# The first layer of one more token group from seven quarter products, and one filler pace for the attention loop

## The chip, the core and the metric

The kernel runs on one NeuronCore of a Trainium2 chip. Its engines run their own instruction streams and meet through semaphores: TensorE (PE in the profile; PEld is its weight loads), VectorE (DVE), ScalarE (ACT), GpSimd (POOL) and SyncE (SP), which here only issues transfers. Products are summed in PSUM, eight banks of 128 partitions by 512 fp32 numbers; VectorE and ScalarE carry results from there to SBUF. The metric is the device time of one execution in microseconds.

## What is computed

Causal attention with a bias per head, then a mixer over tokens (of rank 32) and a mixer over channels, with residuals:

```python
scores = scale * np.matmul(q, k.transpose(0, 1, 3, 2))      # 8 batches, 8 heads, 576 x 576, D = 64
cum = np.cumsum(np.maximum(s, 0.0), axis=-1)
bias = -(cum[:, :, :, None] - cum[:, :, None, :])
scores = np.where(causal, -1e9, scores + np.minimum(bias, 0.0))
x = softmax(scores) @ v                                     # then (batch, 576, 512)
u = x + ((x.transpose(0, 2, 1) @ U) @ V).transpose(0, 2, 1) # U 576 x 32, V 32 x 576
out = u + np.maximum(u @ w_ch1, 0.0) @ w_ch2                # 512 -> 2048 -> 512
```

## The kernel before

**Attention** goes by pairs of heads, n = 0 to 31, four pairs to a batch (b = n // 4). For a pair, `scores` makes the transposed scores in three two-bank PSUM tiles and a small one, ScalarE takes their exponentials (L446, L458, L464), VectorE masks the diagonal blocks (L372), and `values` multiplies with V and divides (L501, L502). From the third batch on, the loop over n interleaves, in the order in which the code is written out, the transposed inputs of pair n+1 (`transposes`, `part_pair`), the scores of pair n and the values of pair n-1.

**`seqmix(b)`** is the token mixer of a batch: 20 small products (L522), a cast, a transpose (L535), a cast, four products against V (L567) and one more group (L592); VectorE adds the residual and writes `uT` (L547). For batches 2 to 6 it runs in the second pair of the next batch (n = 13, 17, 21, 25, 29); for batch 7 after the loop.

**The channel mixer** goes by groups of 512 tokens, g = 0 to 8 (NG = 9), which run across batches. `chanmix(g)` is a generator: sixteen steps of the first layer (`hidden`: four 128x512 products at L662, then a relu at L1044), and then the second layer, `outputs_by_quarters`, in fourteen steps of eight 128x256 products (L720). The second layer is done as a 2x2 block product with seven quarter products instead of eight (p1 to p7, Strassen's way in Winograd's form); sums of weight quarters (B_1 to B_4) and of hidden quarters (A_1 to A_4, L698, in `first_sums` and `total`) are made by VectorE, as are the sums of the products (L734).

**Filler.** The generators wait in the list `fill`. `step_fill` is called after each piece of attention work and adds `pace[1]` to a count; each time this reaches 16, one step of the first generator is issued. `fill_with(n)` issues n steps at once. So pace 12 means 12 steps for 16 calls. There are eight calls to a pair. The loop runs at pace 11 in batch 2, 12 in batches 3 to 5 and 10 in 6 and 7.

**The tail.** After the loop the steps go on until group 6's first layer is issued. Then the attention pools of PSUM are closed, and three others open: two banks for `pwork`, one each for two tiles of the second layer, and four for `hidden_by_quarters`. This function makes the first layer, too, from seven quarter products, for groups 7 and 8: for each of four parts e, 14 slots of which seven do work, four 128x256 products each (L952). Parts overlap: slots 8, 12 and 13 of e stand among the first slots of e+1. ScalarE copies partial sums out and applies relus (L967, L971, L988, L999, L1002, L1006), VectorE adds (L965). Sums of weight quarters (W_1 to W_4, in `first_weight_sums`, L922) are made once, in group 6's first layer; sums of token quarters (`token_sums`, L934 to L937) for each group. Second-layer steps of the group before are placed between the slots by the list `fills`, fourteen for each of groups 7 and 8.

**Order.** TensorE's and GpSimd's instructions stand in the order of the code; on the other engines the scheduler orders them, except where `placed` pins a VectorE instruction behind the one before it. Each engine takes its instructions in that order, so one that waits holds what is behind it.

Of the kernel before, what the change touches and what calls it, by code (L numbers as in the profile page):

```python
# [41 lines left out]
def kernel(  # L42
# [652 lines left out]

    def total(dst, a, b, op, k4):
        at = (slice(None), slice(4 * k4, 4 * k4 + 4))
        nc.vector.tensor_tensor(dst[at], a[at], b[at], op=op)  # L698

# [6 lines left out]
    def outputs_by_quarters(g, hT, u_sd):  # L706
# [146 lines left out]
        for i in halves:  # L853
            product(p6, A_2, B_2, i)
            if i == 1:
                total(A_4, A12, A_2, ALU.subtract, 0)
            yield
        add(U2, U2, p6)
        p5 = bank()
        for i in halves:  # L860
            product(p5, A_1, B_1, i)
            total(*((A_4, A12, A_2), (A_3, A11, A21))[i], ALU.subtract, 1 - i)
            yield
# [3 lines left out]
        for i in halves:  # L867
            product(p3, A_4, B22, i)
            if i == 0:
                o12 = quarter()  # L870
                add_u(o12, o22, 0, 1)
                total(A_3, A11, A21, ALU.subtract, 1)
            yield
# [32 lines left out]

    def first_sum(tile, free):
        return tile.rearrange(free)[:, : 2 * HW].rearrange("p (k n) -> p k n", k=2)

    W_3, W_1, W_4 = (first_sum(slots[i], "p a b -> p (a b)") for i in range(3))  # L910
    W_2 = first_sum(v_slots[2], "p a b c -> p (a b c)")

# [26 lines left out]

    def hidden_by_quarters(u, u_sums, hT, sets):  # L940
        (u11, u21, _, u22), (u_1, u_2, u_3, u_4) = u_quarters(u), u_sums
# [22 lines left out]
        def add(e, r, c, a, b):  # L964
            nc.vector.tensor_tensor(out(e, r, c), a, b, op=ALU.add)  # L965
            if (r, c) == (0, 0):
                nc.scalar.activation(out(e, r, c), out(e, r, c), RELU)  # L967
            elif c == 0:
                both = hT[:, ds(8 + 2 * e, 2), :]
                if sets == 4:  # L970
                    nc.scalar.activation(both, both, RELU)  # L971
                else:
                    nc.vector.tensor_scalar_max(both, both, 0.0)

        parts = {}

        def at(e, slot):
            if not 0 <= e < sets:
                return False
# [11 lines left out]
            if slot == 2:  # L991
                product(p.w, W_3, u_3, e, True)
            elif slot == 3:
                x = two(pwork())
                product(x, W12, u21, e, True)
                add(e, 0, 0, p.p1, x)
            elif slot == 4:
                product(p.y, W_2, u_2, e, False)
                nc.scalar.copy(p.U2, p.y)  # L999
            elif slot == 8:  # L1000
                product(p.y, W_1, u_1, e, False)
                nc.scalar.copy(p.U4, p.y)  # L1002
                add(e, 1, 1, p.U4, p.w)
            elif slot == 12:
                product(p.y, W_4, u22, e, False)
                nc.scalar.activation(out(e, 0, 1), p.y, RELU)  # L1006
            elif slot == 13:
                product(p.w, W22, u_4, e, False)
                add(e, 1, 0, p.U2, p.w)
                if sets == 4 and e in (2, 3):  # L1010
                    first_sums(hT, e == 2)
            return True

        for e in range(sets + 1):
            for slot in range(7):
                late = slot in (1, 5, 6)
                if at(e - late, slot + 7 * late):
                    yield
# [14 lines left out]
    def chanmix(g, hT=None, done=0):  # L1033
        u = uT_of.pop(g)
        if g > 0:
            hT = work.tile([128, NF, 512], BF16, tag="hT", name="hT")
            sums = {1: weight_sums, NG - 3: first_weight_sums}.get(g, lambda: iter(()))()
        for nf in range(done, NF):
# [10 lines left out]
            if g > 0 and nf == 3:  # L1049
                u_sd = by_token(u)  # L1050
            if nf == NF - 1:
                expanded.append(g)
            yield
# [25 lines left out]
    fill = []  # L1079
    expanded = []  # L1080
    relu_by = [E.Activation]
# [3 lines left out]
    def step_fill():  # L1085
        pace[0] += pace[1]
        if pace[0] < 16:
            return
        pace[0] -= 16
        if NG - 3 in expanded and not ps_tail:  # L1090
            return
        while fill:
            if next(fill[0], fill) is not fill:
                return
            fill.pop(0)
# [150 lines left out]
    fill.append(chanmix(1))  # L1246
    pace[1] = 11
    for n in range(2 * PB, NP + 2):
        b, hp = divmod(n, PB)
# [4 lines left out]
        mixing = seqmix(b - 1) if hp == 1 and b > FT else iter(())  # L1254
        if b == B:
            fill_with(3)
            for _ in range(3):
                step(mixing)
                fill_with(2)
        if n > 2 * PB and n + 1 < NP:  # L1260
            for at, _ in enumerate((transposes if n + 1 < ZP else part_pair)(n + 1)):
                step_fill()
                if at == 1:
                    step(mixing)
        if 2 * PB + 1 < n < NP:
            for at, _ in enumerate(scores(n, pT_of(n))):
# [5 lines left out]
        for _ in mixing:  # L1272
            fill_with(1)
        if hp == 1 and FT < b < B:
            fill.append(chanmix(b - 1))
            pace[1] = 12 if b < 6 else 10
        if 2 * PB < n <= NP:
            run(values(n - 1, pT_of(n - 1)))
        if 2 <= b < B - 1:
            if b + 1 < ZB:  # L1280
                load_v(b + 1, range(5 if hp == 0 else 0))
            else:
                load_v(b + 1, ((0, 1), (2,), (3,), (4,))[hp])
    pace[1] = 16
    while NG - 3 not in expanded:
        step_fill()
# [4 lines left out]
    ps_t = ctx.enter_context(tc.tile_pool(name="ps_t", bufs=4, space=bass.MemoryType.PSUM))  # L1291
    tail_sums = {}
    tail_sums[NG - 2] = token_sums(
        uT(NG - 2), v_slots[1].rearrange("p a b c -> p (a b c)")
    )
    xT_again = work.tile([128, 4, 640], BF16, tag="xT", name="xT", bufs=1)
    def hidden_plain(u, hT, nfs):
        for at, nf in enumerate(nfs):
            f1 = pwork()
            hidden(f1, u, nf, range(4))  # L1300
            nc.scalar.activation(hT[:, nf, :], f1, RELU)
            yield

    for g, sets, fills in ((NG - 2, 4, (0, 0, 2, 4, 6, 8, 10, 12, 14, 17, 20, 23, 25, 26)), (NG - 1, 4, (1, 3, 5, 7, 9, 11, 13, 16, 19, 22, 25, 25, 26, 26))):
        u = uT_of.pop(g)
        u_sd = by_token(u, True)
        hT = work.tile([128, NF, 512], BF16, tag="hT", name="hT")
        for at, _ in enumerate(hidden_by_quarters(u, tail_sums[g], hT, sets)):
            for _ in range(fills.count(at)):
                step_fill()  # L1310
            if at == 3 and g < NG - 1:
                tail_sums[NG - 1] = token_sums(
                    uT(NG - 1), xT_again.rearrange("p a b -> p (a b)")
                )
        if sets < 4:
            for one in (True, False):
                first_sums(hT, one)
        while fill:
# [35 lines left out]
```

## Time and profile before

| | |
|---|---|
| median of 3 runs | 347.83 us (347.70 to 348.11) |
| the profiled execution, its own time | 347.92 us |
| its span | 346.1 us |
| PE busy | 336.4 us (97%) |
| DVE busy | 260.6 us (75%) |
| ACT busy | 203.9 us (59%) |
| first-layer products L662 | 407 + 16 rows, 104.2 + 3.9 us busy |
| second-layer products L720 (all forms) | about 880 rows, 273 ns each as recorded |
| quarter products L952 of groups 7 and 8 | 224 rows, 272 to 273 ns each as recorded |

[...] A few per cent of the matmul records are missing, which in a timeline looks like a gap of one product's length. "Idle before" is an engine's idle time just before an instruction, with what ended it. Of an engine beside TensorE, idle time costs nothing by itself.

### The profile page before, as it was taken

What the parts mean: (1) busy time and instruction counts of PE and PEld (TensorE: products, weight loads), DVE (VectorE), ACT (ScalarE), POOL (GpSimd) and SP (SyncE); (2) the same over time, 40 slices, a digit from 0 to 9 for tenths busy, and PEclk for the clock granted to TensorE, in tenths of its full rate; (3) what the DMA queues carried; (4) which work ended last, traced back from release to release, by engine and by line L of the source; (5) the groups of instructions that cost most, each with busy time, mean ns of one, the idle gap of its engine ahead of it and who ended that gap; (6) DMA issues with size and microseconds to landing.
All of it is one profiled execution on the core that took longest, in us unless ns stands there. A gap on an engine that the chain in (4) does not pass through costs nothing.

```text
span 346.1 us, 8930 instructions
## 1 busy us (share of the span) xinstructions
PE 336.4 (97%) x3607; PEld 243.7 (70%) x3641; DVE 260.6 (75%) x576; ACT 203.9 (59%) x308; POOL 125.8 (36%) x183
## 2 busy tenths in 40 slices
PE   8999999999999999999999999999999999999996
PEld 4685556656688558865678568865687568888885
DVE  8894756778799668974898469965988597875874
ACT  4786985638850886178624883388552546665710
POOL 7997358848494309431823374000000000000000
PEclk9999999999999999999999999999999999999999
DMA  7999999999999999999999999495025252010022
GB/s 107 154 180 207 182 185 127 160 204 204 148 167 168 203 138 102 134 196 152 117 117 176 176 128 149 109 179 68 14 56 136 57 95 59 30 63 32 30 93 91
DMA packets 169696, 44.09 MB, mean 127 GB/s; under 512 B 154584, under 2 KB 168024, under 8 KB 169656
## 3 DMA queue, kind: packets, MB, share of 16 engines
q0 software_dynamic: 99440, 18.44, 71.0%
q1 hardware_dynamic: 69928, 24.90, 38.5%
q8 instruction: 28, 0.46, 0.6%
q10 hardware_dynamic: 288, 0.20, 0.2%
q14 instruction: 12, 0.10, 0.1%
HBM read 37.25 MB, written 9.70 MB: 136 GB/s over the span
## 4 chain that ended last, share of the span: by engine, by line
PE 81%; DVE 10%; ACT 4%; issue 3%; DMA 1%; SPq 0%; DVEq 0%; ACTq 0%
PE pwork L662 23%; PE pwork L720 13%; PE quarter L720 10%; PE pscore L428 10%; PE pwork L492 8%; PE parts L952 6%; PE pwork L681 3%; DVE uT L547 2%; DVE slot L698 1%; DVE o_sb L734 1%; DMA slot<-hT 1%; PE pwork L952 1%; PE pscore L662 1%; ACT hT L1044 1%; PE pwork L522 1%
## 5 line engine op out<-in xcount | busy, mean ns | idle before, releaser
L662 PE MATMUL pwork<-uT,w_sb 128*128 128x512 bf16 x407 | 104.2, 379 | 1.9 <-ACT pT L464 0.5
L1044 ACT ACTIVATE hT<-pwork 128x512 bf16<-128x512 f32 x107 | 64.8, 610 | 37.5 <-PE pwork L662 36.6
L446 ACT ACTIVATE pT<-pscore 128x1024 bf16<-128x1024 f32 x57 | 57.5, 1031 | 49.7 <-PE pscore L428 49.4
L662 PEld LDWEIGHTS <-w_sb 128*128 128x128 bf16 x448 | 39.2, 98 | 38.8 <-issue 1.0
L121 POOL DMA_DIRECT2D qk_sd<-in_q_dram x46 | 34.3, 746 | 71.8 <-DMA qk_sd<-qk_sd 34.6
L428 PE MATMUL pscore<-slot 68*128 68x128 bf16 (+1 forms) x506 | 55.8, 245 | 0.8 <-DMA slot<-hT 0.6
L428 PEld LDWEIGHTS <-slot 68*128 68x128 bf16 x570 | 42.2, 97 | 18.5 <-DMA slot<-hT 0.8
L720 PEld LDWEIGHTS <-hT 128*128 128x128 bf16 x496 | 46.7, 98 | 7.2 <-DVE uT L547 0.5
L372 DVE TENSOR_TENSOR pT<-pT,keep 128x512 bf16<-128x512 bf16 (+1 forms) x81 | 28.7, 355 | 27.7 <-ACT pT L446 21.0
L492 PEld LDWEIGHTS <-pT 128*128 128x128 bf16 x870 | 32.5, 97 | 6.2 <-issue 0.9
L178 POOL DMA_DIRECT2D v_slot<-in_v_dram x40 | 34.0, 862 | 5.7 <-DMA w_sb<-in_moe_w_ch_dram 5.2
L492 PE MATMUL pwork<-v_slot,pT 128*128 128x65 bf16 x870 | 35.4, 193 | 0.2 <-DVE uT L547 0.2
L121 POOL DMA_DIRECT2D qk_sd<-in_k_dram x46 | 33.7, 733 | 1.5 <-DMA v_slot<-in_v_dram 1.3
L502 DVE TENSOR_TENSOR x_sb<-pwork,rec 128x320 bf16<-128x320 f32 x64 | 31.2, 489 | 1.4
L458 ACT ACTIVATE pT<-pscore 128x1024 bf16<-128x1024 f32 x29 | 30.3, 1046 | 2.7 <-PE pscore L428 2.6
L720 PE MATMUL pwork<-w_sb,hT 128*128 128x256 bf16 x240 | 29.9, 273 | 0.0
L720 PEld LDWEIGHTS <-slot 128*128 128x128 bf16 x256 | 24.1, 98 | 4.1 <-issue 1.1
L335 DVE COPY slot<-pwork 64x576 bf16<-64x576 bf16 x27 | 21.7, 803 | 3.5 <-PE pwork L316 1.8
L501 DVE RECIPROCAL rec<-pwork 128x5 f32<-128x5 f32 x64 | 12.1, 190 | 12.1 <-PE pwork L492 11.4
L720 PE MATMUL pwork<-w_sum,slot 128*128 128x256 bf16 x160 | 20.1, 273 | 0.3 <-DVE o_sb L734 0.3
L720 PE MATMUL quarter<-w_sb,hT 128*128 128x256 bf16 x144 | 18.0, 273 | 0.3 <-DVE uT L547 0.3
L362 DVE COPY slot<-qk_sd 64x1152 bf16<-64x1152 bf16 x30 | 16.3, 542 | 0.3
(164 smaller groups left out, 486.9 us busy)
## 6 DMA issues: line engine op xcount, KB each, us to landing
out_dram<-o_sb SPq DMA_DIRECT2D x34, 256.0 KB
v_slot<-in_v_dram POOLq DMA_DIRECT2D x32, 128.0 KB, 6.4
w_sb<-in_moe_w_ch_dram POOLq DMA_DIRECT2D x4, 1024.0 KB, 13.3
qk_sd<-in_q_dram POOLq DMA_DIRECT2D x46, 72.0 KB, 4.4
qk_sd<-in_k_dram POOLq DMA_DIRECT2D x46, 72.0 KB, 4.6
qk_sd<-in_q_dram POOLq DMA_DIRECT2D x5, 144.0 KB, 5.1
qk_sd<-in_k_dram POOLq DMA_DIRECT2D x5, 144.0 KB, 5.2
qk_sd<-in_q_dram POOLq DMA_DIRECT2D x2, 288.0 KB, 9.1
```

Source lines behind the costliest of these rows:

```text
L121: nc.gpsimd.dma_start(out=of_pair(n)[:, c, :, hh, :], in_=src[b, 2 * hp + hh].rearrange("(t p) d -> p t d", p=TR),)
L178: nc.gpsimd.dma_start(out=vt[:rows_t, t, :, 0:D], in_=v[b, :, ds(t * 128, rows_t), :].rearrange("h p d -> p h d"),)
L372: nc.vector.tensor_tensor(dst, dst, keep[:, :, 0:w].to_broadcast([128, n_tiles, w]), op=ALU.min)
L428: nc.tensor.matmul(dst, lhsT=slot[0:KA, hh, ds(S + j * 128, 128)], rhs=slot[0:KA, hh, lo:hi], start=True, stop=True,)
L446: nc.scalar.activation(pT[:, hh, 0:1024], near, EXP, scale=scale)
L458: nc.scalar.activation(pT[:, :, 1024:1536], mid.rearrange("p (a b) -> p a b", a=2), EXP, scale=scale)
L492: nc.tensor.matmul(po[:, i, :], lhsT=pT[:, hh, ds(place(j, i), 128)], rhs=vt[:, j, h, :], start=(j == 0), stop=(j == i), skip_group_check= ...
L502: nc.vector.tensor_tensor(x_sb[:, hp, :, ds(hh * D, D)], po[:, :, 0:D], rec.to_broadcast([128, 5, D]), op=ALU.mult,)
L662: nc.tensor.matmul(f1, lhsT=w1_sb[:, kt, ds(nf * 128, 128)], rhs=u[:, kt, :], start=(kt == 0), stop=(kt == 3),)
L720: nc.tensor.matmul(acc[:, i, :], lhsT=a[:, kt, ds(i * 128, 128)], rhs=b[:, kt, :], start=(begin and i == 0 and kt == 0), stop=(kt == HF - ...
L952: nc.tensor.matmul(acc[:, i, :], lhsT=w[:, kt, ds((2 * e + i) * 128, 128)], rhs=m[:, kt, :], start=(begin and i == 0 and kt == 0), stop=(k ...
L1044: nc.scalar.activation(hT[:, nf, :], f1, RELU)
```

## The change

Group 6's first layer leaves `chanmix`, and `hidden_by_quarters` makes it in the tail, woven with what is left of group 5's second layer, as groups 7 and 8 are woven with the second layers of 6 and 7.

- The point at which the PSUM pools change (`seam`) moves forward: from the end of group 6's first layer to the middle of group 5's second layer, after p6. Group 5's p5, p3, p7 and p4 then take banks from the new two-bank `pwork`. Eight of its steps are left; they go behind slots 0, 3, 7, 11, 14, 18, 22 and 25 of group 6's 28.
- The weight sums W_1, W_3 and W_4 lie in a buffer of the q and k loads that is free from batch 3 on, instead of the slots of the scores. They are made two at a time behind the values of pairs 25, 26, 28 and 29. Group 6's token sums are made in n = 30, in another part of these buffers; group 7's move from ahead of the tail into group 6's slots, pinned in order, as group 8's are into group 7's.
- Group 5's A sums after p6 are pinned too.
- The pace is 10 from batch 2 to the end. The loop ends at n = 31; the values of pair 31 follow directly, with one filler step behind each half, and then `seqmix(7)`.
- Both branches for fewer than four parts in `hidden_by_quarters` go, as they weren't taken.

```diff
@@ outputs_by_quarters
         add(U2, U2, p6)
+        if g == NG - 4:
+            seam.append(g)
+            yield
         p5 = bank()
@@ where the sums lie
-    W_3, W_1, W_4 = (first_sum(slots[i], "p a b -> p (a b)") for i in range(3))
+    W_3, W_1, W_4 = (
+        qk_sd[(ZB + 1) % 2][:, ds(2 * S + i * 2 * HW, 2 * HW)].rearrange("p (k n) -> p k n", k=2)
+        for i in range(3)
+    )
@@ step_fill
-        if NG - 3 in expanded and not ps_tail:
+        if seam and not ps_tail:
             return
@@ the loop
-    pace[1] = 11
-    for n in range(2 * PB, NP + 2):
+    pace[1] = 10
+    first_weights = first_weight_sums()
+    tail_sums = {}
+    for n in range(2 * PB, NP):
...
-        if hp == 1 and FT < b < B:
+        if hp == 1 and FT < b < B - 1:
             fill.append(chanmix(b - 1))
-            pace[1] = 12 if b < 6 else 10
-        if 2 * PB < n <= NP:
-            run(values(n - 1, pT_of(n - 1)))
+        if n == NP - 2:
+            placed(
+                lambda: tail_sums.update({NG - 3: token_sums(uT(NG - 3), qk_sd[ZB % 2])})
+            )
+        if 2 * PB < n:
+            for _ in values(n - 1, pT_of(n - 1)):
+                step_fill()
+                if n - 1 in (25, 26, 28, 29):
+                    step(first_weights)
...
+    for _ in values(NP - 1, pT_of(NP - 1)):
+        fill_with(1)
+    mixing = seqmix(B - 1)
+    fill_with(1)
+    for _ in range(2):
+        step(mixing)
+        fill_with(2)
+    for _ in mixing:
+        fill_with(1)
     pace[1] = 16
-    while NG - 3 not in expanded:
+    while not seam:
         step_fill()
@@ the tail
-    for g, sets, fills in ((NG - 2, 4, (0, 0, 2, 4, 6, 8, 10, 12, 14, 17, 20, 23, 25, 26)), (NG - 1, 4, (1, 3, 5, 7, 9, 11, 13, 16, 19, 22, 25, 25, 26, 26))):
+    for g, fills in (
+        (NG - 3, (0, 3, 7, 11, 14, 18, 22, 25)),
+        (NG - 2, (0, 0, 2, 4, 6, 8, 10, 12, 14, 17, 20, 23, 25, 26)),
+        (NG - 1, (1, 3, 5, 7, 9, 11, 13, 16, 19, 22, 25, 25, 26, 26)),
+    ):
...
             if at == 3 and g < NG - 1:
-                tail_sums[NG - 1] = token_sums(
-                    uT(NG - 1), xT_again.rearrange("p a b -> p (a b)")
+                placed(
+                    lambda: tail_sums.update(
+                        {g + 1: token_sums(uT(g + 1), sums_in[g + 1])}
+                    )
                 )
```

## The prediction

> **What bounds the kernel now.** I read the page first: engines, slices, chain of waits.
>
> ```profile
> PE 336.4 (97%) x3607; PEld 243.7 (70%) x3641; DVE 260.6 (75%) x576; ACT 203.9 (59%) x308; POOL 125.8 (36%) x183
> ...
> PE   8999999999999999999999999999999999999996
> ...
> PEclk9999999999999999999999999999999999999999
> ...
> PE 81%; DVE 10%; ACT 4%; issue 3%; DMA 1%; SPq 0%; DVEq 0%; ACTq 0%
> ```
>
> TensorE is busy in every slice, at full granted clock, and carries 81% of the chain: a product taken away is time won, and a wait put before TensorE is time lost. Because matmuls overlap, the length of a row is not its cost; the spacing of starts in the timeline is (columns: start us, length us, engine, line):
>
> ```profile
> 196.03 1.89 PE L662 MATMUL pwork<-uT,w_sb 128*128 128x512 bf16 x8
> 197.76 0.58 PE L428 MATMUL pscore<-slot 68*128 68x128 bf16 x5
> ...
> 307.52 0.60 PE L952 MATMUL parts<-xT,v_slot 128*128 128x256 bf16 x4
> 307.96 1.04 PE L720 MATMUL quarter<-w_sb,hT 128*128 128x256 bf16 x8
> ```
>
> Eight 128x512 products in 1.73 us are 0.216 each; four 128x256 in 0.44 are 0.109. Next, where TensorE waits today: around the end of the seventh seqmix, in the seqmix of n=29, and once in the tail.
>
> ```profile
> 238.58 1.94 ACT L446 ACTIVATE pT<-pscore 128x1024 bf16<-128x1024 f32 x2 [0.35 <-PE pscore L428]
> 240.40 0.60 ACT L1044 ACTIVATE hT<-pwork 128x512 bf16<-128x512 f32 x1
> 240.88 1.05 ACT L458 ACTIVATE pT<-pscore 128x1024 bf16<-128x1024 f32 x1
> 241.20 0.39 PE L567 MATMUL pscore<-V_sb,ux 32*128 32x512 bf16 x2
> 241.78 0.31 ACT L464 ACTIVATE pT<-pwork 128x128 bf16<-128x128 f32 x1
> 242.14 2.75 PE L662 MATMUL pwork<-uT,w_sb 128*128 128x512 bf16 x11 [0.55 <-ACT pT L464]
> ...
> 277.09 0.39 PE L567 MATMUL pscore<-V_sb,ux 32*128 32x512 bf16 x2
> 278.30 1.28 DVE L547 TENSOR_TENSOR uT<-pscore,xT 128x128 bf16<-128x128 f32 x2
> 279.50 1.74 DVE L547 TENSOR_TENSOR uT<-pwork,xT 128x64 bf16<-128x64 f32 x5
> 280.30 0.29 PE L592 MATMUL pwork<-V_end,ux 128*128 128x64 bf16 x4
> 281.29 0.94 PE L720 MATMUL quarter<-w_sb,hT 128*128 128x256 bf16 x7 [0.27 <-DVE uT L547]
> ...
> 319.70 0.59 ACT L1006 ACTIVATE hT<-parts 128x512 bf16<-128x512 f32 x1
> 320.34 0.60 PE L952 MATMUL parts<-uT,w_sb 128*128 128x256 bf16 x4
> ```
>
> All three are waits for a PSUM bank that a slower engine has not emptied. In lost starts: 0.72 us at 242.14 (ready at 241.42), 0.28 and 0.43 at 280.30 and 281.29, 0.16 at 320.34. The rows also give what the engines take back to back: VectorE's seven L547 fill 278.30 to 281.25, and four L922 of 0.685 fill 2.49 us (at 265.36), so one such 1024-element sum, and likewise a 128x512 sum that reads PSUM, costs 0.60; ScalarE's 128x1024 exponential 0.91, its 128x512 copy or relu 0.48, 128x512 relu in SBUF 0.53, the 128x1024 one 0.96. A consumer starts 0.20 (VectorE) to 0.22 us after the last product's slot ends, TensorE 0.05 after a consumer ends.
>
> **The change, part by part.**
>
> *Products.* 64 of 128x512 go (64 x 0.216 = 13.8), 112 of 128x256 come (112 x 0.109 = 12.2): -1.6 us, all on TensorE's path. Elsewhere the TensorE work is the same. [...]
>
> *The old seam* (0.28 + 0.43) is gone where it stood: group 7's start now has no seqmix ahead of it. -0.7.
>
> *The new seam.* In the changed program's order TensorE does L567 of the seventh seqmix, three half-products of group 5 (2.62), L592 (0.12), the second half of p6 (0.87), group 6's first quarter product (0.44), then the first half of p5. Group 5 now draws p5, p3, p7, p4 from the new pool of two banks, shared with group 6's W12 products, and p5's bank is the one p6 was in: it waits for VectorE's U2 += p6. VectorE's order between L567 and that sum: six L547 (2.52), o11's first add (0.60), the seventh L547 (0.33), o11's second add, one A_4 sum (0.60 each), then U2 += p6 (0.69 to its end): 5.34, with both handovers 5.59. TensorE gets there in 4.05. Wait: 1.54.
>
> *Group 6's quarters.* Take the start of p6's second half as t=0 and go on through the listed order with the durations above. (a) VectorE, held by that wait, then has group 7's four token sums, which moved here (4 x 0.335), and two A sums before the adds that free group 6's banks: the add for x(e=1) ends at 9.83, the relu behind it in ScalarE's order at 10.4, the relu that empties y(e=0) at 10.99. TensorE reaches y(e=2) at 9.86: wait 1.19. Before, a piece of second layer stood between slots 13 and 0; with eight pieces instead of fourteen there is none, so even with VectorE idle the relu costs 0.22 + 0.59 + 0.05 against one product of 0.44, about 0.4. (b) y(e=3): 16.60 against 15.87, wait 0.73. (c) the last W22 product needs the (1,1) add of e=3: 23.65 against 23.17, 0.48. Sum with the seam 3.9. A check by work: from t=0 VectorE has 31 sums at 0.60, six token sums and one L547: 20.9 us, in a stretch whose products take 20.5; today's group 7 has 19.9 in 26.6. So VectorE becomes the bound of this stage. Bounds: 2.3 (seam and two bare relu waits) to 5. I take 3.9.
>
> *ScalarE here*: 16 relus (7.7) go, 24 operations come (13.7 in 20.5 us): not a bound by itself; its order behind VectorE is in (a).
>
> *Fewer filler steps.* Pace 10 of 16 gives five steps per n where batches 3 to 5 had six (batch 2: 5.5): TensorE's period is 1.37 + 0.87 + 5 x 0.862 = 6.55 instead of 7.41 us. ScalarE needs 3 x 0.91 + 0.28 + 5 x 0.48 = 5.4 of it, VectorE in second-layer periods up to 6.5 (two masks, copies, divisions 2.57, five steps of about 0.73). What goes wrong then is the seqmix period: with hidden-layer filler the row at 242.14 repeats, as exp, exp, relu, exp, small exp outlast the products. n=17, 21 and 25 get that alignment now: 3 x 0.72, where today they lose 0.31 (at 139.15), 1.25 (170.14 to 178.35) and 0: +0.6. n=29 moves from that kind to the second-layer kind, whose four cases today (n=13, 17, 21, 25) lose 0.68, 0.31, 1.25, 0, mean 0.56: -0.2. Each hidden stretch at this pace also lost 0.14 once (235.25), now in three more groups: +0.4. Values of n=31 follow at once; their mult ends 0.2 after the last seqmix products want it: +0.2. Together +1.0. Bounds: -1 (no wait at the four seqmix) to +3 (VectorE at its limit through n=27 to 29).
>
> *Moved sums.* The eight weight sums (4.8) leave group 6's hidden steps, where VectorE waited 1.20 at a time, for n=26, 27, 29, 30. VectorE's work there by the order: n=27 6.4 and n=28 6.5 of 6.55, n=29 10.6 of 11.6: nothing on TensorE as long as that holds; if not, it is in the +3. Group 6's four token sums stand in n=30 (5.2 of 6.55): nothing. The placed flag of group 5's sums only fixes their order.
>
> *SyncE, DMA, POOL.* Group 6's transpose by tokens (2.20 on SP at 264.67) now goes ahead of batch 7's four L509 transposes, none of which it delays, as it waits for n=29's data only; the last L509 has about 2 us to spare. Loads must come in 6.55 us periods: a turned pair is copied some 13 us after its issue on SP (207.16 to 223.31): covered.
>
> Sum against the profiled execution, 347.92 (span 346.1): -1.6 - 0.7 + 3.9 + 1.0 = +2.6, so 350.5; the median of the three runs, 347.83, is 0.1 lower, within a run's scatter. I say 350.5.
>
> **The rivals.**
>
> *Faster: VectorE is never late.* For: it is 75% busy over the span and sits at 19.9 of 26.6 in today's tail. Then p5 finds its bank free, only two bare relu waits stay (0.9), n=29 loses nothing: -1.6 - 0.7 + 0.9 + 0.3 = 346.8. It decides at U2 += p6: this must be done 1.5 us sooner than its queue allows. 0.10.
>
> *No change.* The seam wait is there, but without the backlog after it (tail 2.4, attention 0): 348.0. Against: the 20.9 us in 20.5. 0.13.
>
> *Slower still: VectorE bounds n=27 to 29* at 98% with the weight sums, and seqmix 6 waits for its casts: +2 on the forecast, 352.8. For: 170.14, the same kind of wait. 0.11.
>
> *Loads become the bound*: the period stays at 7.4 for 12 of the n: about 358. Against: no TensorE wait on a DMA after 20 us. 0.02.
>
> [...] 0.02.
>
> **How the numbers follow.** Forecast 0.62, own range 349.0 to 352.4. About 0.2% is what a measurement of this kernel can tell from no change (347.1 to 348.5). The range 347.9 to 352.9 leaves out the faster case, half of no change and the last two. Faster 0.10, same 0.13, slower 0.77.
>
> **What would show it.** In the trace after: TensorE's busy time no longer than before less 1.6; the first L721 of p5 idle before it 1 to 1.6 us, ended by VectorE's U2 sum; waits before y(e=2) and y(e=3) of group 6 ended by ScalarE's relu; VectorE over 90% from there to group 7; waits ended by ScalarE after L567 at n=17, 21, 25. Wrong it would be by a p5 that starts at once, or by seqmix periods without a wait.

## The result, and the profile after

The changed kernel takes 362.89 us (median of six runs, 361.88 to 365.28); beside it the kernel before took 347.85 (347.49 to 348.38). The ratio is 1.044, with a 95% interval of 1.040 to 1.048: 15 us slower, where 2.6 us were forecast and 352.9 was the upper end of the range. The sign was right, the size was not. The profiled execution of the changed kernel took 362.15 us (span 360.4), 14.2 more than that of the kernel before.

The page of the changed kernel: the engines, TensorE's slices, its granted clock, the chain.

```profile
PE 339.3 (94%) x3657; PEld 250.0 (69%) x3689; DVE 270.2 (75%) x594; ACT 208.5 (58%) x314; POOL 126.3 (35%) x183
...
PE   8899999999999999998889979999998899999996
...
PEclk9999999999999999999898999999999999999999
...
PE 64%; DVE 15%; DMA 10%; ACT 5%; issue 3%; POOL 1%; SPq 1%; DVEq 0%; ACTq 0%; POOLq 0%
```

Two things are new against the kernel before. DMA carries 10% of the chain, where it carried 1%. And TensorE has slices below nine, each 9 us wide, inside the attention loop: three from 162 to 189 us and one at 207, with the granted clock below full in the slices at 171 and 189. The stage that the prediction spent most of its length on, group 6, has only two, from 270 to 288.

To put numbers on it, TensorE's products in the program's order were each given the spacing that the prediction reads from the rows (0.216 us for a 128x512, 0.109 for a 128x256, and so on), and what the time between two points exceeds their sum is lost time (the levels depend by up to about 1 us on how these spacings are taken, the differences between kernels by up to 0.5). The products sum to 331.5 us before and 329.9 after. Lost, in us, by stretch of each profiled execution:

| kernel | 1 to 100 | 100 to 160 | 160 to 262 | 262 to the end |
|---|---|---|---|---|
| before | 6.3 | 0.9 | 1.6 | 1.1 |
| after | 6.4 | 1.1 | 13.9 | 4.4 |
| after less before | +0.1 | +0.2 | +12.3 | +3.3 |

Together 15.9, less 1.6 of products, is 14.3, the difference of the two spans. The tail was forecast at 3.9 - 0.7 = 3.2 and measures 3.3. The loop was forecast at 1.0 and has twelve and a half. In the tail, the timeline of TensorE in the changed kernel (start us, length us, what, idle before and its releaser):

```profile
273.98 1.03 PE L721 MATMUL pwork<-w_sum,slot 128*128 128x256 bf16 x8 [1.28 <-DVE U L735]
282.21 0.60 PE L960 MATMUL parts<-uT,w_sb 128*128 128x256 bf16 x4 [1.08 <-ACT hT L1011]
287.75 0.60 PE L960 MATMUL parts<-uT,w_sb 128*128 128x256 bf16 x4 [0.57 <-ACT hT L1011]
294.79 0.60 PE L960 MATMUL parts<-qk_sd,w_sb 128*128 128x256 bf16 x4 [0.32 <-DVE hT L973]
```

These are the four waits that the prediction listed, at the places it named. In lost starts they are 1.44, 1.25, 0.74 and 0.48; it had 1.54, 1.19, 0.73 and 0.48.

What VectorE waited for between 160 and 250 us, longest in total first (us in total, times, longest):

```profile
DVE uT L547 <- DMA xT<-x_sb: 5.9, 2, 3.1
...
DVE slot L362 <- PE pscore L428: 3.6, 1, 3.6
```

Neither wait is in the kernel before: among VectorE's waits there, none of a seqmix sum is for a transposed x, and none is at a copy of a turned pair. The first is the seqmix sum (L547) that needs the DMA transpose of a pair's x. It stood before the values at 172.34 (2.20 us lost on TensorE) and at 212.16 (2.44). SyncE's queue ahead of the first one, with VectorE and TensorE at its end:

```profile
152.74 5.15 SPq L1033 DMA_TRANSPOSE u_sd<-uT  x1
157.98 0.59 SPq L745 DMA_DIRECT2D out_dram<-o_sb  x1
158.67 1.64 SPq L509 DMA_TRANSPOSE xT<-x_sb  x1
160.48 4.65 SPq L350 DMA_TRANSPOSE qk_sd<-qk_sd  x1
165.19 1.65 SPq L296 DMA_DIRECT2D slot<-rows_hbm  x3
166.94 1.23 SPq L509 DMA_TRANSPOSE xT<-x_sb  x1
```

```profile
171.52 1.09 DVE L547 TENSOR_TENSOR uT<-pwork,xT 128x256 bf16<-128x256 f32 x3 [2.81 <-DMA xT<-x_sb]
...
172.34 0.78 PE L492 MATMUL pwork<-v_slot,pT 128*128 128x65 bf16 x15 [2.04 <-DVE uT L547]
```

Pair 19's x was ready at 161.07; its transpose was issued at 166.94, after a transpose by tokens that held SyncE for 5.15 us and a turned pair that held it for 4.65. In the kernel before the same transpose was issued 0.03 us after its x (170.11). The order of SyncE's queue has changed, too: the planner orders SyncE as it does VectorE. The batch's transpose by tokens (L1033) stands ahead of the x of pairs 17 and 21 in the kernel before, and of pairs 18 and 23 in the changed program, so nearer to the last x, on which the seqmix waits.

The second wait comes with a change of VectorE's order. These are VectorE's copies of turned pairs in the changed program (place in the list of VectorE's instructions, runs of equal ones merged; line; tile written and landing read; slot0 with qk_sd0 is pair 23, slot2 with qk_sd1 pair 25, slot1 with turned pair 24):

```
285 L362 TensorCopy slot0_96<-qk_sd0_70 64x1152
291 L362 TensorCopy slot0_96<-qk_sd0_70 64x1152
298 L362 TensorCopy slot2_98<-qk_sd1_71 64x1152
305 L362 TensorCopy slot1_97<-turned_139 64x1152 x2
317 L362 TensorCopy slot2_98<-qk_sd1_71 64x1152
```

The first copy of pair 25 stands ahead of both copies of pair 24; further down the first copy of pair 30 stands ahead of those of pair 29. In the kernel before all copies are in pair order. Nothing in the change asks for it: the planner orders VectorE by its own estimate, and the shorter loop changed its choice. VectorE's timeline there, and TensorE's:

```profile
180.92 0.69 DVE L698 TENSOR_TENSOR hT<-hT 128x1024 bf16<-128x1024 bf16 x1
185.24 0.46 DVE L362 COPY slot<-qk_sd 64x1152 bf16<-64x1152 bf16 x1 [3.64 <-PE pscore L428]
...
187.61 1.27 DVE L362 COPY slot<-turned 64x1152 bf16<-64x1152 bf16 x2
188.91 0.69 DVE L735 TENSOR_TENSOR o_sb<-o_sb,pwork 128x512 f32<-128x512 f32 x1
```

```profile
187.74 0.22 PE L428 MATMUL pwork<-slot 68*128 68x64 bf16 x2 [0.20 <-DVE x_sb L502]
189.65 0.95 PE L492 MATMUL pwork<-v_slot,pT 128*128 128x65 bf16 x15 [1.69 <-DVE o_sb L735]
```

VectorE has nothing to do for 3.64 us. The profile names the scores, and the expectations below follow it, but those that read slot2 (pair 22's) had ended by 180.78; what came last is pair 25's turned data, which landed at 185.15 (SyncE had issued the transpose from 178.28 to 180.52). In e1_token_late and e5_before_pace10 the same wait is put down to this transfer. So the copy stood in VectorE's order before its data could be there. Behind it stood divisions, second-layer sums and the copies of pair 24. TensorE lost 2.4 us from 186 to 189.7.

Both waits cost twice. The stretches behind them, by window (TensorE's granted clock is the third number from the end):

```profile
172.30:176.00 3.70, 3.44 (x35) 2.29 (x37) 3.56 (x9) 0.60 (x1) 3.70 (x6) 0.55 1.27 82
189.60:193.20 3.60, 3.55 (x40) 2.98 (x40) 2.71 (x8) 0.00 (x0) 0.00 (x0) 0.53 2.13 138
212.10:216.00 3.90, 3.78 (x46) 2.42 (x48) 2.52 (x8) 1.31 (x3) 0.00 (x0) 1.00 2.30 163
```

Behind the first and the second wait the granted clock stood at 0.5 for 3.41 us (172.66 to 176.07 and 189.72 to 193.14 on the clock's own track), which lost 1.7 us each time; behind the third, the longest, it stayed at 1.00. So the 13.9 us of the loop are, within half a microsecond: 2.2 + 1.7 at 172, 2.4 + 1.7 at 187, 2.4 at 212, 0.7 each at 166 and 206 (the seqmix waits for ScalarE that were forecast), and 2.6 from 232 to 262.

### The profile page after: what moved, and what is told of

Same layout as the page of the kernel before. It is cut to its first block, busy times and chain, and to the rows that moved or that the text cites. A ratio compares the mean times of both kernels' runs of the same rounds, so it can differ in the third digit from the quotient of the medians.

```text
span 360.4 us, 9068 instructions
## 1 busy us (share of the span) xinstructions
PE 339.3 (94%) x3657; PEld 250.0 (69%) x3689; DVE 270.2 (75%) x594; ACT 208.5 (58%) x314; POOL 126.3 (35%) x183
## 4 chain that ended last, share of the span: by engine, by line
PE 64%; DVE 15%; DMA 10%; ACT 5%; issue 3%; POOL 1%; SPq 1%; DVEq 0%; ACTq 0%; POOLq 0%
PE pwork L662 14%; PE pwork L721 10%; PE quarter L721 10%; PE pscore L428 7%; PE pwork L492 7%; PE parts L960 7%; DMA xT<-x_sb 3%; PE pwork L681 3%; DVE o_sb L735 3%; DMA qk_sd<-qk_sd 2%; DMA v_slot<-in_v_dram 2%; DVE uT L547 2%; ACT pT L446 1%; DVE hT L973 1%; DVE slot L362 1%
## 5 line engine op out<-in xcount | busy, mean ns | idle before, releaser
L662 PE MATMUL pwork<-uT,w_sb 128*128 128x512 bf16 x345 | 90.5, 382 | 3.4 <-ACT pT L464 1.7
L446 ACT ACTIVATE pT<-pscore 128x1024 bf16<-128x1024 f32 x57 | 55.9, 1027 | 42.5 <-PE pscore L428 42.5
L1049 ACT ACTIVATE hT<-pwork 128x512 bf16<-128x512 f32 x89 | 53.6, 608 | 44.5 <-PE pwork L662 43.7
L662 PEld LDWEIGHTS <-w_sb 128*128 128x128 bf16 x384 | 33.9, 98 | 34.2 <-issue 3.3
L428 PE MATMUL pscore<-slot 68*128 68x128 bf16 (+1 forms) x506 | 54.0, 245 | 1.1 <-DMA slot<-hT 0.9
L428 PEld LDWEIGHTS <-slot 68*128 68x128 bf16 x570 | 41.3, 97 | 18.2 <-issue 1.2
L492 PEld LDWEIGHTS <-pT 128*128 128x128 bf16 x870 | 33.5, 99 | 14.1 <-DVE uT L547 5.3
L492 PE MATMUL pwork<-v_slot,pT 128*128 128x65 bf16 x870 | 36.8, 196 | 6.2 <-DVE uT L547 4.5
L458 ACT ACTIVATE pT<-pscore 128x1024 bf16<-128x1024 f32 x29 | 30.2, 1041 | 1.4 <-PE pscore L428 1.4
L721 PE MATMUL pwork<-w_sum,slot 128*128 128x256 bf16 x160 | 21.1, 280 | 1.8 <-DVE U L735 1.3
L973 DVE TENSOR_TENSOR hT<-pT,parts 128x512 bf16<-128x512 f32 x24 | 16.3, 683 | 8.0 <-PE parts L960 4.9
```

Source lines behind the costliest of these rows:

```text
L428: nc.tensor.matmul(dst, lhsT=slot[0:KA, hh, ds(S + j * 128, 128)], rhs=slot[0:KA, hh, lo:hi], start=True, stop=True,)
L446: nc.scalar.activation(pT[:, hh, 0:1024], near, EXP, scale=scale)
L458: nc.scalar.activation(pT[:, :, 1024:1536], mid.rearrange("p (a b) -> p a b", a=2), EXP, scale=scale)
L492: nc.tensor.matmul(po[:, i, :], lhsT=pT[:, hh, ds(place(j, i), 128)], rhs=vt[:, j, h, :], start=(j == 0), stop=(j == i), skip_group_check= ...
L662: nc.tensor.matmul(f1, lhsT=w1_sb[:, kt, ds(nf * 128, 128)], rhs=u[:, kt, :], start=(kt == 0), stop=(kt == 3),)
L721: nc.tensor.matmul(acc[:, i, :], lhsT=a[:, kt, ds(i * 128, 128)], rhs=b[:, kt, :], start=(begin and i == 0 and kt == 0), stop=(kt == HF - ...
```

## The experiments

Three theories stood at the start. O (order): two queues stand in a bad order, SyncE behind the transpose by tokens and VectorE behind a copy that came too early; each can be mended with the pace left alone. P (pace): ten steps of sixteen make a loop that is too short for transfers and VectorE whatever the order. And a rival to both: the moved sums, the values' steps or group 6's quarters bring the loss, and the pace does not. After the first four runs a fourth theory, M (margin), took the place of P.

**e5_before_pace10.** The kernel before with the pace alone changed.

```
-    pace[1] = 11
+    pace[1] = 10
...
-            pace[1] = 12 if b < 6 else 10
+            pace[1] = 10
```

> The kernel before with nothing changed but the pace, ten sixteenths throughout (11 and 12 in batches 2 to 5 before); the steps left over are done after the loop. It tells whether the 12.3 us that the changed kernel lost from 160 to 262 us come with the pace alone. Both O and P: yes, 357 to 361 us, with waits on L547 and at the copies in the same places. If the moved sums, the values' steps or group 6's quarters bring them instead: 347.5 to 351.

Measured: 358.84 us (357.31 to 362.0), ratio 1.031 (1.022 to 1.039). From 160 to 262 us it loses 11.9, as against 13.9 in the changed kernel and 1.6 before. The copies of pairs 25 and 30 stand ahead in this program too, and VectorE's waits from 100 to 250 us have both groups:

```profile
DVE uT L547 <- DMA xT<-x_sb: 4.4, 1, 4.4
...
DVE slot L362 <- DMA qk_sd<-qk_sd: 4.3, 1, 4.3
```

So the fewer filler steps bring nearly all of the loop's loss by themselves; the sums, the values' steps and group 6's quarters are not needed for it.

**e1_token_late.** The transpose by tokens later, where its buffer has long been free.

```
-            if g > 0 and nf == 3:
+            if g > 0 and nf == 8:
                 u_sd = by_token(u)
```

> The changed kernel with one number altered: a group's transpose by tokens (L1033) is issued after hidden step 8 instead of step 3. Theory O (order): in the changed kernel SyncE stood behind this transpose, which waits for VectorE's last reader of the one u_sd tile (152.74 to 157.28 and 200.91 to 202.98), and so issued the xT transposes of pairs 19 and 23 late; VectorE's seqmix sums (L547) waited 2.8 and 3.1 us, TensorE 2.20 and 2.44 and then ran slower for some 1.7. With SyncE never behind it both waits go: 357 to 358.5 us, and the values of n=20 and n=24 start without a wait on L547; the waits at 187 to 196 us stay. Theory P (pace): the loop at ten sixteenths is too short for the transfers, whose landing is what is late; the transposes come late again from another place: 361.5 to 363.

Measured: 362.82 us (361.08 to 363.25), ratio 1.040 (1.033 to 1.047): nothing is won. SyncE's queue in front of pair 19's transpose in this kernel:

```profile
155.09 1.33 SPq L509 DMA_TRANSPOSE xT<-x_sb  x1
156.59 3.88 SPq L350 DMA_TRANSPOSE qk_sd<-qk_sd  x1
160.53 5.48 SPq L1033 DMA_TRANSPOSE u_sd<-uT  x1
166.11 1.03 SPq L296 DMA_DIRECT2D slot<-rows_hbm  x2
167.25 1.74 SPq L509 DMA_TRANSPOSE xT<-x_sb  x1
```

The transpose by tokens waits for nobody now (VectorE has freed its tile), and still holds the queue for 5.48 us, the turned pair before it for 3.88. The x waits as long as before, 5.8 us against 5.9, and VectorE's two waits for such transposes come to 6.7 us against 5.9. That half of O falls: SyncE is not behind VectorE, its transposes themselves take longer to issue than in the kernel before, where those of pairs and of x take 1.2 to 2.7 us and those by tokens into `u_sd` 2.2 to 3.8. Why, no run here settles; GpSimd's loads are landing meanwhile (the DMA engines' share over 160 to 175 us is 1.60 in this run, packets of several queues counted), but they are in the kernel before as well (1.39). The edit did not take the transpose by tokens out of the way either: it now stands directly ahead of pair 19's x. A queue with this transpose behind the last x was not tried.

**e2_copies_in_order.** The other half of O: a copy must stand behind the copy before it, the pace left at ten.

```
+            pair_copies.append(last_on(E.DVE))
+            if len(pair_copies) > 1:
+                after(tc, pair_copies[-1], pair_copies[-2])
```

> The changed kernel with one thing added: each copy of a turned pair (L362) must stand behind the copy before it in VectorE's order. In the changed kernel the first copies of pairs 25 and 30 stand ahead of those of pairs 24 and 29; VectorE waited 3.6 us at the first of them (181.61 to 185.24) for scores that still read the slot, TensorE lost 2.5 us from 186 to 190 and 1.5 more at a lower clock up to 196. Theory O (order): this goes, and perhaps up to 1 us of the 2.3 lost from 232 to 250: 357.5 to 359. Theory P (pace): VectorE is late there because it has too much to do in 6.55 us, and its order matters little: 361.5 to 363.

Measured: 354.28 us (352.41 to 356.95), ratio 1.019 (1.009 to 1.029), 8.6 less than the changed kernel; more than theory O gave. VectorE from 180 to 188 us, where the changed kernel had its gap:

```profile
180.95 0.91 DVE L367 COPY slot<-turned 64x1152 bf16<-64x1152 bf16 x2
181.90 0.69 DVE L743 TENSOR_TENSOR o_sb<-o_sb,pwork 128x512 f32<-128x512 f32 x1
...
187.39 1.01 DVE L367 COPY slot<-qk_sd 64x1152 bf16<-64x1152 bf16 x2
```

Pair 24 is copied at 180.95, pair 25 at 187.39, and nothing waits. From 186 to 196 us the profiled run (352.76) loses 0.1 where the changed kernel lost 4.0. Pair 30's copy was worth less: the waits around the sixth seqmix, where it had stood ahead, go from 2.66 to 2.04. But the run also has no wait at 172, and 0.73 instead of 2.44 before the values of the seqmix at n=25, though the edit leaves the transposes in the same order on SyncE; and its runs lie 4.5 us apart. So 4.0 of the 8.6 stand where the copy stood, and part of the rest is something that differs from run to run.

**e3_both.** The two edits together.

> The changed kernel with both: the transpose by tokens after step 8, and the copies in pair order. Theory O: the losses add up, 362.2 - 4.7 - 4 - 0.5 = 352 to 354.5; what is left over the kernel before is the tail (3.3) and the hidden kind of seqmix. Theory P: waits of the same sum turn up at other places of the loop, 358 or more.

Measured: 355.83 us (353.07 to 356.78), ratio 1.020 (1.011 to 1.028): between the two ranges, and no different from e2_copies_in_order, as the first edit is worth nothing. Its profiled run shows yet another transfer late, a load of V, issued at 100.57 and landed at 109.15:

```profile
109.20 0.19 PE L500 MATMUL pwork<-v_slot,pT 128*128 128x65 bf16 x1 [2.23 <-DMA v_slot<-in_v_dram]
```

In the kernel before the same load landed at 102.65, 5 us ahead of its values. This led to theory M: at 6.55 us a period the transfers are not always late, but no spare time is left, and chance decides which one is.

**f1_pace_11_8.** Copies in order, and longer periods while pairs are still loaded.

```
-    pace[1] = 10
+    pace[1] = 11
...
+            pace[1] = 11 if b < 6 else 8
```

> The changed kernel with the copies in pair order (as e2_copies_in_order), and the filler at 11 of 16 up to n=24 and 8 from n=25 on (about as many steps in all), so that the periods in which pairs are still loaded are longer and those behind the last load shorter. Theory M (margin): e2_copies_in_order's four times from 352.4 to 357.0 differ because its loads and transposes now land with no time to spare at 6.55 us; at 7.0 the times agree within 1.5 us, at 351 to 353, with no wait of TensorE above 0.8 us from 100 to 230 us. Theory O alone (only the order of the copies mattered): the same scatter as e2_copies_in_order. Theory V (VectorE bounds the short periods behind n=25, with the weight sums in them): the wait moves there, 353 to 356.

Measured: 353.29 us (352.47 to 354.29), ratio 1.015 (1.011 to 1.019). The runs lie 1.8 us apart instead of 4.5 (M had said 1.5, and 351 to 353). From 160 to 230 us it loses 1.3 (e2_copies_in_order 2.5), and no sum of a seqmix waits for a transposed x, in this profile or in those of h1, j1, j2, k1 and l2, all at 11 or 12 up to n=24; l3, at 12, has one such wait of 0.5 us. In the profiles at pace ten there is such a wait each time: 5.9 us in all in the changed kernel, 6.7 in e1, 1.4 in e2, 1.1 in e3, 4.4 in e5, 4.7 in g1_tail. That fits M, but it does not show it, for the planner changed SyncE's order with the pace once more: in all programs at ten the second of the two transposes by tokens stands directly ahead of pair 23's x, in f1, h1, j1 and j2 ahead of pair 22's, and in k1, l2 and l3 ahead of pair 21's, as in the kernel before. In f1 this transpose holds SyncE even longer than any in the changed kernel, and no sum waits, since pair 22's x is the one behind it, and pair 23's (203.85) still comes in time:

```profile
191.05 6.45 SPq L1041 DMA_TRANSPOSE u_sd<-uT  x1
...
203.85 1.84 SPq L517 DMA_TRANSPOSE xT<-x_sb  x1
```

So longer periods and another order on SyncE are not told apart here; that the order alone does not decide it is seen in e2_copies_in_order, which has the changed kernel's order of transposes and no wait at 172. The gain is spent behind n=25, as theory V said: TensorE waits 1.17 us for VectorE's division in n=25's seqmix, and 2.26 instead of 1.44 at p5's bank.

**g1_tail.** Copies in order at pace ten, group 6's pieces placed anew, group 7's token sums later.

```
-        (NG - 3, (0, 3, 7, 11, 14, 18, 22, 25)),
+        (NG - 3, (1, 3, 6, 10, 13, 17, 21, 24)),
...
-            if at == 3 and g < NG - 1:
+            if at == (20 if g == NG - 3 else 3) and g < NG - 1:
```

> The changed kernel with the copies in pair order, and two edits in group 6's stage: its eight pieces of second layer at steps 1, 3, 6, 10, 13, 17, 21, 24 (one stands between the last W22 product of a part and the next y), and group 7's four token sums after step 20 instead of 3. If the stage's waits come from what VectorE has ahead of U2's sum and from a relu with no piece to cover it: p5's wait falls from 1.44 to 0.1 to 0.7, the waits for y from 1.24 and 0.73 to 0.5 and less; 2 to 3 us less than e2_copies_in_order in the stage. If the stage is bound by VectorE's total there (20.9 us against 20.5 of products), only the 1.3 us of the token sums is won.

Measured: 353.09 us (352.23 to 354.2), ratio 1.014 (1.008 to 1.019). After 262 us it loses 3.2 instead of 4.6. The two waits for y are gone (0.16 is left of 1.98), p5's is 1.00, and a new one of 0.89 stands at a product behind the token sums. That fits a relu with no piece of second layer over it, but the token sums, which had stood ahead of the adds that these relus need, were moved in the same run, so which of the two edits took the waits away is open; and with 1.4 us the stage won about what the token sums take, as the second theory said.

**h1_pace_and_tail.** All three.

> All of it: copies in pair order, pace 11 then 8, and group 6's stage as in g1_tail. With M and the relu cover right: 348 to 350.5, no slower than the kernel before by more than 1%; with V: 351 to 353.

Measured: 351.15 us (350.96 to 351.71), ratio 1.009 (1.006 to 1.012). It is the fastest with group 6 in quarters, 11.7 us below the changed kernel, its runs 0.8 us apart, and still 3.4 us above the kernel before, in the range that theory V gave. Losses: 2.9 from 160 to 262, 4.1 behind it. The largest single wait is the first bank of the new pool:

```profile
264.21 1.03 PE L729 MATMUL pwork<-w_sum,slot 128*128 128x256 bf16 x8 [1.66 <-DVE uT L555]
```

VectorE works there without a gap, on the sums of the seventh seqmix and of group 5.

**j1_later_piece, j2_sums_on_pool, k1_pace_12_6.** Two kinds of attempt at that wait, which both miss what was expected. j1 puts p5's first half two quarter products later and the token sums after step 12:

```
-        (NG - 3, (1, 3, 6, 10, 13, 17, 21, 24)),
+        (NG - 3, (3, 4, 6, 10, 13, 17, 21, 24)),
```

> As h1_pace_and_tail, but the piece with p5's first half stands after group 6's step 3 instead of 1 (two quarter products, 0.87 us, more ahead of it) and group 7's token sums after step 12 instead of 20. If p5's wait (1.82 us in h1_pace_and_tail) is only VectorE's queue ahead of U2's sum, it falls to 0.8 to 1.0, and the 0.89 us at the last W12 product goes or moves to a y by less: 349 to 350.5. If VectorE's total bounds the stage, the waits only move: 351.

Measured: 352.59 us (352.31 to 353.9), ratio 1.014 (1.012 to 1.017), slower than h1. The same 1.82 us now stand before the first W12 product, which draws from the same pool, and the wait at a later product of the stage grew from 0.89 to 1.75: the waits moved and grew.

j2 gives the eight weight sums and group 7's four token sums to GpSimd (k1 does so too, with the pace 12 and then 6):

```
-                    lambda: nc.vector.tensor_tensor(dst[:, k, :], a[:, k, :], b[:, k, :], op=op)
+                nc.gpsimd.tensor_tensor(dst[:, k, :], a[:, k, :], b[:, k, :], op=op)
```

> As j1_later_piece, but group 7's four token sums and the eight weight sums are made by GpSimd, which has nothing to do after the last load. If VectorE's total is what bounds group 6's stage and n=26 to 30, this takes 1.3 us there and 4.8 us before: 347.5 to 349. If GpSimd and VectorE slow each other down (VectorE's sums longer than 0.685 us while GpSimd works), or its sums come too late for the first W_3 product: 350 to 355.

> As j2_sums_on_pool with the filler at 12 from batch 3 on, as in the kernel before, and 6 from n=25. Theory M says that up to n=24 it then loses what the kernel before lost (0.6 us less from 160 to 230 than h1_pace_and_tail, no 0.72 at n=17 and 21); behind n=25 ScalarE needs 4.5 of 4.8 us: 346 to 348.5 if j2_sums_on_pool gains, 349 to 351 if periods of three steps are bound by another engine.

Measured: 365.08 us (363.07 to 366.36) and 365.79 (364.33 to 369.01), ratios 1.048 (1.043 to 1.053) and 1.053 (1.047 to 1.059). GpSimd's sums take 2.4 us each, and VectorE's slow down while they run. VectorE's groups from 212 to 224 us in j2 (busy us, mean ns of one):

```profile
L706 DVE TENSOR_TENSOR hT<-hT 128x1024 bf16<-128x1024 bf16 x1 | 2.7, 2675 | 0.0
...
L510 DVE TENSOR_TENSOR x_sb<-pwork,rec 128x320 bf16<-128x320 f32 x2 | 1.0, 476 | 0.0
```

and in j1, where GpSimd only loads:

```profile
L510 DVE TENSOR_TENSOR x_sb<-pwork,rec 128x320 bf16<-128x320 f32 x4 | 1.9, 482 | 0.0
...
L706 DVE TENSOR_TENSOR hT<-hT 128x1024 bf16<-128x1024 bf16 x1 | 0.6, 648 | 0.0
```

The sum between SBUF tiles takes 2.68 us instead of 0.65; the one that reads PSUM is unchanged. Part of the loss is clock: in j2 10.2 us and in k1 17.1 us of the loop ran at half the granted clock.

**l2_seam_after_p5, l3_pace_12_6.** The sums back on VectorE, twelve up to n=24 as in the kernel before, then 7 or 6, and the pools changed after p5 (the same three lines go from behind p6, and seven pieces stand at 3, 6, 10, 13, 17, 21, 24).

```
-            pace[1] = 11 if b < 6 else 8
+            pace[1] = 12 if b < 6 else 7
...
         add(o22, U2, p5)
+        if g == NG - 4:
+            seam.append(g)
+            yield
         p3 = bank()
```

> As h1_pace_and_tail, with the filler at 12 from batch 3 to n=24, as in the kernel before, then 7; and with the place at which the pools change after p5 instead of after p6 (seven pieces left for group 6's stage, at steps 3, 6, 10, 13, 17, 21, 24). Theory M: up to n=24 the losses of the kernel before (about 0.6 us less than h1_pace_and_tail from 160 to 230, none of the two 0.72). If the wait for the first bank of the new pool (1.8 us) is VectorE's queue of the seventh seqmix, it stays, less the one product more that lies over it (0.9); behind n=25 VectorE with the weight sums has 1.2 us more per n than its 4.4: 348.5 to 350.5. If the loop's short end is bound by VectorE: 351 to 353.

> The same with 6 instead of 7 from n=25: three pieces less in the loop's last n, three more around the seventh seqmix, where VectorE is what TensorE waits for. If that wait is worth more than what the shorter periods cost: 347.5 to 349.5, less than l2_seam_after_p5; if the short periods are bound by VectorE or ScalarE, 1 to 3 us more than it.

Measured: 355.17 us (354.16 to 358.49) and 353.2 (352.41 to 353.96), ratios 1.022 (1.017 to 1.028) and 1.014 (1.011 to 1.017). Both are above what was expected. From 100 to 230 us they lose 2.4 and 1.9, h1 3.4 over the same, and the two 0.72 are gone, as M said; but from 160 to 230 us, the stretch that l2's expectation named, l2 loses some 0.7 more than h1, and l3 as much as h1. Behind 262 us they lose 8.9 and 6.7: the wait for the first bank of the new pool stays at 1.97 and 1.88, wherever the pools change, and the last waits of the stage, 0.9 and 0.4 in h1, are 1.5 and 0.9 in both. Three steps more around the seventh seqmix (l3 against l2) go with about 2 us less, the sign that l3's expectation had; but 1.7 of it is one stretch at half clock less (two in l2, at 266.03 and 286.51, and one in l3, at 284.93). No arrangement tried brings group 6's quarters below the kernel before.

## Why the prediction was wrong

**Right: the products.** 331.5 us of products against 329.9. The 336 quarter products (L960) of the changed kernel start 0.109 us apart (median), as the 224 before did. The sign announced for it, TensorE's busy time, was a bad one: it rose from 336.4 to 339.3, since it adds modelled lengths, those at half clock among them.

**Right: the tail.** Forecast +3.2, measured +3.3, with each of the four waits within 0.1 us and with its releaser. One reason given was too strong: VectorE was to be over 90% busy from p5 to group 7; it was busy 17.8 of 23 us from 272 to 295. It is late in places, not bound throughout. (One slip stands among the rivals: the last, the 0.02 for smaller products that together cost no less than the larger ones, without the gain of 1.6 us and so at 352.1, lies inside the range that is said to leave it out. Nothing hangs on it.)

**Right: the hidden kind of seqmix.** 0.72 us at n=17, 21 and 25 (134.65, 166.57, 206.16), ended by ScalarE's small exponential, and the waits of 0.14 in the values.

**Wrong: "Fewer filler steps", its bounds of -1 to +3, and with them "SyncE, DMA, POOL ... covered".** Of 12.3 us more from 160 to 262, the step had 1.0. It failed in two ways.

First, it added up what each engine has to do in a period of 6.55 us and took VectorE's order as it was. VectorE's order is not written out; the planner makes it, and at pace ten it put two copies ahead of their turn. e5_before_pace10 has the same two copies ahead with nothing but the pace changed, and e2_copies_in_order puts them in order and wins 8.6 us, 4.0 of them where the first copy stood. The change of order stands in the program and could have been read there before any run, the second copy within the stretch (n=27 to 30) of which the prediction says that VectorE's work fits.

Second, "covered" rested on the time between a turned pair's issue and its copy (some 13 us, it says; its own two rows, 207.16 and 223.31, are 16.2 apart), and on no wait of TensorE for a DMA. The transfer that became late was another: x's transpose. In the kernel before 6.8 us lay between the end of pair 19's issue (171.40) and the sum of the seqmix that reads it (178.21), and a turned pair was seen by GpSimd to land 2.1 to 6.8 us after its issue: there was nothing to spare for a later issue. In the changed kernel the issue came 5.87 us after the x was ready, behind transposes that held SyncE for 5.15 and 4.65 us, and the data landed 3.3 us after it. The rival "Loads become the bound" was given 0.02 and spoke of a period that stays at 7.4; what came is a loop that runs at its new period and loses 2 us here and there. That the pace brings this is shown by e5_before_pace10. Whether it does so by the shorter period (M) or by SyncE's order is argued and not shown: f1_pace_11_8 changed both, and its time lies within the scatter of e2_copies_in_order.

**Not counted at all: the clock.** Two waits of 2.2 and 1.85 us were each followed by 3.41 us at half clock, 1.7 us lost apiece, 3.4 of the 12.3. Every wait in the prediction had been priced at its own length.

What stays open: why SyncE needs 4 to 6.5 us to issue a transpose at some places, which of the transfers in flight delays the landing, and what another order of SyncE's queue alone would win at pace ten.

## What to carry to other kernels

Where a planner orders an engine, a change of pace is a change of order: compare the order of the two programs on every engine through the whole loop, and look for instructions that must wait long where they now stand, before adding up times. For a transfer that nothing waits for today, reckon the spare time (from when its source is ready to its first reader, less what stands ahead of it in the issuing queue and the longest landing seen), since that is what a shorter loop spends. Where the profile says what ended a wait, see when that one was done: here the named scores had read the slot 4.5 us earlier. And a wait can cost more than its length: 2.4 us before 189.65 were followed by 1.7 lost to the clock.

## What the runs showed of the hardware

TensorE's granted clock fell to 0.5, for 3.41 us at a time, behind (or in the last tenths of) waits of 2.20 and 1.85 us in the changed kernel, 1.86 in e1_token_late, 1.85 and 3.75 in e5_before_pace10, 2.39 in e3_both, 1.97 in l2_seam_after_p5, and 1.49 with 0.9 behind it in l2_seam_after_p5 and l3_pace_12_6; in j2 and k1 also for two and three times as long. It did not fall behind waits of 2.44 us in the changed kernel, 1.86 and 3.43 in e1_token_late, 2.26 in f1_pace_11_8, 1.88 in l3_pace_12_6, or 1.82 in h1_pace_and_tail. So the length of a wait alone does not decide it. Where it lies counts, too: in each profile the changes of the clock between the first rise and the end lie a whole number of 3.41 us apart (172.66, 176.07, 189.72 and 193.14 in the changed kernel). Cut each profile into pieces at that spacing and add up the starts that TensorE lost in each piece at full clock: the clock was at 0.5 right behind each of the 12 pieces that lost 2.08 us or more, behind none of those that lost 1.91 or less, and behind one of the two that lost 2.00 (from 241.44 in j2, not from 210.20 in the changed kernel). The 3.43 us in e1_token_late were cut into 1.7 and 1.8. So a wait of 1.85 us was enough for it and one of 3.43 was not. What sets the 3.41 us, no run here shows.

A VectorE sum between bf16 tiles in SBUF took 2.5 to 2.7 us in j2_sums_on_pool while GpSimd made sums of its own, of 2.3 to 2.5 us (means), instead of 0.65 to 0.69 in j1_later_piece: 1.8 to 2.0 us more. A division, with one of its inputs in PSUM, kept its 0.48. Why the one grows and the other does not, no run here shows.
